# Batch 0 of a fused attention and feed-forward kernel: softmax with tokens on the partitions, sums of k and v two heads at a time, the first weights by columns

## The chip, the cores and the metric

The kernel runs on one core of one Trainium2 chip. The metric is the device time of one execution in microseconds, as the median of the runs shown. Engines are named as in the profile: PE (TensorE, matrix products), DVE (VectorE), ACT (ScalarE), POOL (GpSimd), SP (SyncE, which here only issues loads and stores).

## The reference

```
# q, k, v: 8 batches x 8 heads x 576 x 64; phi: 8 x 8 x 576 x 32; all float32
a = exp(phi - max(phi, axis=2));  a = a / (sum(a, axis=2) + 1e-9)     # softmax over the 576
k_m = einsum('bhsm,bhsd->bhmd', a, k);  v_m = einsum('bhsm,bhsd->bhmd', a, v)
s = (q @ k_m^T) / sqrt(64)                                            # 576 x 32 for each head
attn = exp(s - max(s, axis=-1));  attn = attn / (sum(attn) + 1e-9)    # softmax over 32 memory slots
x = (attn @ v_m), heads side by side                                  # 4608 x 512
h = x @ w_in                                                          # w_in 512 x 2048
out = max(0.01 * h, h) @ w_out                                        # w_out 2048 x 512
```

w_in and w_out arrive as 64-bit floats.

## The kernel before

**What is computed in which order.** For each batch the kernel sums k and v over the 576 positions with the weights exp(phi - max), which leaves 32 memory slots a head. It doesn't form attn @ v_m: v_m is multiplied into w_in first (the fold, `fold_products`), so that a token's 8 x 32 probabilities are multiplied by a folded matrix of 256 x 2048 straight away. The output is computed in units of tokens: `up_products` (L1248 early, L1378 later), the leaky relu, and `down` (L1335, later L1446) with w_out.

**Layout.** A batch has 8 heads in two groups `g` of four (`hh`). Positions lie on the partitions as 64 rows a group and nine columns `j` (KJ = 9, of which the first NJ = 6 are called early here). The array of PE is used in tiles: a product of 64 rows by 32 columns takes one of eight tiles, and products on different tiles run side by side. float32 products take two passes each.

**Order of the work.** All work is cut into named steps, and the strings OPENING and LATER list them. Every engine executes its share in that order. A step waits for what it reads and for the buffers that it writes. There are three kinds of PSUM buffers (`pa` three, `ph` two, `po` three banks). Loads go into eight slots of one arena in turn (`ld_slot`), or, for batch 0, into tiles that get their weights only later; eight semaphores are shared by the loads in turn.

**The steps of batch 0** (prefix `a0.`), with the lines of the profile before:

- `phi`, `k`, `v`, `q`: loads, from SP's queue, two of phi from ACT's. `T`: an exp of one column (L566), which brings ACT's table load with it. `z.n`: n idle products (L1538) into a fresh `po` tile; they compute nothing that is used.
- `A1` maximum of phi over positions (DVE L622), `A2` its transpose on PE (L663) and the maximum `mx` (L670), `A3` the identity scaled by mx, one half on DVE (L672), one on ACT (L673), `B0` PE spreads these over the partitions (L679), `B1` subtraction (DVE L688), `B2` exp (ACT L694), `B3` sums of the exponentials (DVE L710 to L719).
- `C10` sums of k (PE L738), `C11` sums of v (same line), `C2` and `C30` the divisor `r`, `C3k` and `C31` scaling to `x_k` (ACT L780) and `x_v` (ACT L810), `C4` a bound of x_v for later scalings.
- `D10`, `D3`: transposes of x_k (PE L833) and their copy to `kT` (ACT L868); `D11`, `D5`: the same for v (`vT`, L874). `R` and `Q`: transposes of q on PE (L933) and copies (DVE L942, ACT L944). `E10` to `E13`: scores (PE L979).
- `E2`: 32 x 32 transposes of the scores on DVE (L1030), so that the memory slots lie along the free axis; `S01` to `S08`: softmax over the slots, with a maximum (L1057), subtraction (L1060), exp (ACT L1065), sum (L1069 to L1071), product (L1074) and a second 32 x 32 transpose to `a` (L1082). `S1x` does the late positions.

`i0` to `i3` and `o0` to `o3` are quarters of w_in and w_out: `ld` loads a piece, `h` and `y` or `t` convert it (ACT L406 and L395, DVE L415, the put). `f0j.1` is the fold of quarter j (PE L1156), `f0j.2` its copy (ACT L1521), `u0.P0` the first product of tokens with folded weights. Batch 1 has its steps `a1.` spread among the units.

Of the kernel before, what the change touches and what calls it, by code (L numbers as in the profile page):

```python
# [31 lines left out]
EPS = 1e-09  # L32
# [7 lines left out]
a0.phi1 a0.phi2 z.2 z.2 z.2 z.2 z.2 a0.A12 a0.phi0 a0.phi3 a0.T a0.k3 a0.A10 a0.A11 z.2 z.2 a0.A13  # L40
a0.A2 a0.A3 z.2 a0.B0 a0.B11 z.2 z.2 a0.k2 a0.k0 a0.B10 z.2 a0.k1 z.2 a0.B21 a0.B20 a0.B12 a0.B30
a0.q3 a0.B31 a0.q1 a0.B22 a0.C100 a0.C101 a0.B32 a0.C102 a0.R3 a0.C2 a0.C30 a0.q2 a0.q0 a0.R1 a0.Q3
a0.C3k a0.R2 a0.Q2 i0.ld1 a0.Q1 a0.D10 a0.D3 a0.R0 a0.Q0 a0.E10 i0.y1 a0.E11 i0.h1 z.2 a0.E21 i0.ld0
z.2 z.2 i0.y0 a0.E20 z.2 z.2 a0.v0 z.2 a0.S01 a0.v1 z.2 a0.v2 z.2 a0.S02 a0.v3 i0.ld2 i0.h0 a0.C11
i0.t1 a0.S03 z.2 a0.q4 a0.q5 i0.t0 o0.ld1 o0.ld0 z.2 i1.ld0 a0.C31 i0.y2 a0.S04 a0.D11 a0.R5 i0.h2
a0.D5 a0.R4 a0.Q5 a0.S05 i1.ld1 i0.t2 a0.S06 a0.Q4 f00.1 a0.E12 f00.2 a0.E13 a0.C4 u0.P0 a0.E22 i0.b
u0.V0 u1.P0 a0.D2 o0.y0 u1.V0 u0.P1 u1.P1 o0.h0 a0.E23 o0.h1 i1.ld2 o0.ld2 a0.S11 i1.h0 o0.y1 o1.ld0
o1.ld1 u1.V1 a0.S12 a0.S13 i1.y0 u0.V1 o0.t0 a0.D4 i1.y2 i1.h1 i1.y1 o0.t1 o0.y2 o1.ld2 o0.h2 u0.O0
a0.S14 a0.S15 u1.O0 i1.h2 i1.t0 o2.ld0 a0.S16 o1.y0 o1.y1 o1.h0 i1.t1 i2.ld0 i1.t2 u0.O1 i2.ld1
f01.1 o0.t2 o1.h1 o1.t0 o1.y2 f01.2 u1.O1 i2.ld2 o1.h2 o1.t1 o2.y0 i2.h0 o1.t2 i2.h1 o2.ld1 u2.P0  # L50
u3.P1 a1.phi o2.ld2 a1.kv0 i2.y0 u2.V0 u2.P1 o2.h0 i2.y1 i2.y2 i2.h2 u2.V1 i2.t0 o2.y1 o2.t0 i2.t1
i2.t2 u2.O0 u3.V1 o2.h1 f02.1 a1.A1 f02.2 u3.P0 a1.kv1 o2.h2 a1.A2 u3.V0 a1.A3 o2.y2 a1.kv2 a1.kv3
u4.P1 o1.b o2.t1 a1.B0 a1.B10 a1.B20 u3.O0 a0.S17 u4.P0 i2.b o2.t2 a1.B3 i3.ld0 i3.h0 a1.C10 u4.V0
o0.b a1.C2 a1.C30 a1.q0 u2.O1 a1.C31 a1.q1 i3.ld1 a1.C3k i3.y0 i3.ld2 a1.D11 a1.D10 u4.V1 a1.D5
a0.S18 a1.C4 a1.D3 a1.D2 u5.P0 a1.Q0 a1.D4 u3.O1 i3.t0 o3.ld0 a1.Q1 i3.h1 a1.E1 a1.E20 i1.b u5.P1
u5.V0 o2.b o3.ld2 i3.y1 a1.E21 u4.O0 i3.y2 a1.S01 u5.O0 i3.h2 a1.S02 u5.V1 a1.E22 o3.y0 a1.S03 i3.t1
i3.t2 o3.h0 a1.S04 f03.1 o3.ld1 o3.y2 i3.b o3.h2 ci.1 a1.S11 u4.O1 a1.S05 o3.y1 a1.S06 o3.h1 o3.t0
a1.S12 o3.t2 f03.2 ci.2 o3.t1 a1.S13 o3.b a1.S07 u7.P0 ci.3 a1.S14 ci.4 u7.V0 w1.1 e. co.1 u6.P0
co.2 co.3 w0.2 a1.S08 u6.V0 u6.P1 co.4 e2. u7.P1 w1.2 a1.S15 a1.S16 u6.V1 o0.k2 u6.O0 u7.V1 u7.O0
o0.k0 o0.l0 u5.O1 o0.k1 o0.l1 u6.O1 a1.S17 a1.S18  # L60
# [10 lines left out]
o0.l2 u7.O1 W01.h1 a2.phi a2.kv2 a2.kv1 o0.s0 W01.h0 a2.A1 Z0.0 o0.s1 a2.kv0 a2.A2 W01.l0 o0.m0  # L71
W01.l1 o0.m1 o0.n0 o0.n1 Z0.1 o0.s2 i0.k1 W11.p Z0.2 P8.0 P8.1 V8.0 a2.kv3 W11.h1 P9.0 o0.s3 V8.1
# [114 lines left out]
def kernel(  # L187
# [96 lines left out]
    for g in range(2):  # L284
        nc.gpsimd.memset(sides[g * 64:(g + 1) * 64, g:g + 1], 1.0)
    junk = wi[0].bitcast(BF16)[:, 0:WC]
# [77 lines left out]
    w_out_v = w_out.rearrange("(j p f) e -> j p (f e)", p=P, j=NQ)  # L364
    PIECES = [(c0, min(PC, WC - c0)) for c0 in range(0, WC, PC)]

    def weights(kind, j, steps, act):
# [4 lines left out]
        src, dst, split, col = src[j], dst[j + 1], split[j], slice(col, col + 1)  # L372
# [3 lines left out]
        def load(i):  # L376
# [3 lines left out]
            if kind == "o":  # L380
                nc.sync.dma_start(st[:, 0:n], src[:, c0:c0 + n])
                x = c0 + n
# [27 lines left out]
        def put(i):  # L410


            hi, lo, _ = words.pop(i)
            c0, n = PIECES[i]
            nc.vector.scalar_tensor_tensor(  # L415
                dst.bitcast(U32)[:, c0:c0 + n], hi, 3, lo, ALU.logical_shift_left, ALU.bitwise_or
            )
# [100 lines left out]
    def attention(b, steps, chunks, f32_chunks=0):  # L518
# [29 lines left out]

        def load_kv(hh, kinds):
            if ("ld", hh) not in ld:  # L550
                n = 4 * 2 * KJ * D
                t = ld["ld", hh] = (
                    (wo[2], wo[3], wo[4], wi[4])[hh] if b == 0
                    else ld_slot() if b == 1 else at(n * hh, n)
                )
                ld["kv", hh] = t[:, 0:2 * KJ * D].rearrange("p (i j d) -> p i j d", i=2, j=KJ)
# [32 lines left out]
        def load_pairs(x):  # L589
            hs, js = (slice(x, x + 1), slice(0, NJ)) if x < HP else (  # L590
                slice(2 * x - 2 * HP, 2 * x - 2 * HP + 2), slice(NJ, KJ)
            )
            s = hs.start // 2
            if ("q", s) not in ld:
                ld["q", s] = ld_slot()[:, 0:2 * KJ * D].rearrange(
                    "p (hh j d) -> p hh j d", hh=2, j=KJ
                )
# [103 lines left out]
        def sum_phi(x):  # L701
# [6 lines left out]
            t = wi[3][:, n:n + HP * 2 * M].rearrange("p (hh j m) -> p hh j m", hh=HP, j=2)  # L708
            if x == 0:
                nc.vector.tensor_tensor(t[:, :, 0], ph[:, :, 0], ph[:, :, 1], ALU.add)  # L710
                return
            if x == 1:
                nc.vector.tensor_tensor(t[:, :, 1], ph[:, :, 2], ph[:, :, 3], ALU.add)
                nc.vector.tensor_tensor(t[:, :, 0], t[:, :, 0], ph[:, :, 4], ALU.add)
                return
            s0 = var["s0"] = att.tile([P, HP, M], F32, name="r1k", bufs=2)
            for j in (5, 7):
                nc.vector.tensor_tensor(t, t, ph[:, :, j:j + 2], ALU.add)
            nc.vector.tensor_tensor(s0, t[:, :, 0], t[:, :, 1], ALU.add)  # L719
# [7 lines left out]
        def slots_of(kinds, js=range(KJ)):  # L727
# [5 lines left out]
            cs = slice(kinds[0] * D, (kinds[-1] + 1) * D)  # L733
            for j in js:
# [18 lines left out]
        def _():  # L753
            s0 = var["s0"].rearrange("p hh m -> p (hh m)")
            if b == 0:
                nc.tensor.matmul(var["pk"][0][:, P:P + NG], s0, sides, start=True, stop=True)
# [5 lines left out]
        def _():  # L762
            var["r2"] = r = sm.tile([P, NG], F32, name="r2")
            sums_ = var["pk"][0][:, P:P + NG]
# [9 lines left out]
        def _():  # L774
            x_k = att.tile([P, NG, ND, NB, 32], F32, name="x_k")
            if b == 0:
                flat = x_k.rearrange("p g db tb x -> p (g db tb x)")
                var["x_k"] = flat[:, 0:NG * P].rearrange("p (g i d) -> p g i d", g=NG, i=2)
                for g in range(NG):
                    nc.scalar.activation(  # L780
                        var["x_k"][:, g],
                        var["pk"][g][:, 0:D].unsqueeze(1).broadcast_to([P, 2, D]),
                        AF.Copy, scale=var["r2"][:, g:g + 1],
# [41 lines left out]
        def _():  # L825
# [4 lines left out]
            if b == 0:  # L830
                var["pkT"] = pkT = ps_a.tile([P, NG, P], F32, name="pa")
                for g in range(NG):
                    nc.tensor.transpose(  # L833
# [804 lines left out]
```

## Time and profile before

| | us |
|---|---|
| median of 3 runs | 653.81 |
| lowest and highest | 653.44, 656.79 |
| the profiled execution, time | 656.04 |
| the profiled execution, span | 654.2 |
| PE busy in it | 637.7 |
| DVE busy | 513.3 |
| ACT busy | 393.8 |
| first product of tokens (u0.P0) | 28.49 |

The span is the profiled part of one execution, from its first to its last instruction. Busy is time in which an engine had an instruction in work; idle products count as busy, and a view by stretches and the chain of waits show where PE works for nothing. The clock granted to PE was full throughout.

### The profile page before, as it was taken

The page shows a single profiled execution, that of the slowest core. Times are in us where ns is not written, and L with a number is a line of the kernel's source. Part 1 is how long each engine was busy: PE and PEld are TensorE (multiplying, and loading weights), DVE is VectorE, ACT ScalarE, POOL GpSimd, SP SyncE. Part 2 cuts the span into 40 slices and gives each one's busy share as a digit, 9 for nine tenths or more (in the row PEclk, how much of TensorE's full clock was granted, in tenths as well). Part 3 has the DMA queues.
Part 4 walks back from the last instruction along what each step waited for, and adds up shares of the span by engine and source line. Part 5 has one row for each costly group of instructions (what it writes and reads, how often), then busy time and mean ns, then how long its engine had stood idle before and what let it go on. Part 6 is the DMA issues. An engine that isn't in the chain of part 4 may idle for free.

```text
span 654.2 us, 17243 instructions
## 1 busy us (share of the span) xinstructions
PE 637.7 (97%) x7317; PEld 482.8 (74%) x7317; DVE 513.3 (78%) x856; ACT 393.8 (60%) x682; POOL 30.1 (5%) x41
## 2 busy tenths in 40 slices
PE   8999999999999999999999999999998999999997
PEld 4545445665546778888888888887877888889896
DVE  4677898998987898899869975789886897575641
ACT  4599977764554555467546665655574466564543
POOL 0000130000010001002000010000010001000000
PEclk9999999999999999999999999999999999999999
DMA  9899814014602644421253011164114010010102
GB/s 319 320 367 317 289 36 122 10 22 89 193 10 36 136 142 82 120 88 41 35 130 127 3 32 42 26 120 146 33 27 79 12 33 18 17 28 7 33 1 50
DMA packets 85885, 61.17 MB, mean 93 GB/s; under 512 B 62128, under 2 KB 69040, under 8 KB 85808
## 3 DMA queue, kind: packets, MB, share of 16 engines
q1 hardware_dynamic: 85328, 59.64, 32.4%
q8 instruction: 57, 0.93, 0.6%
q10 hardware_dynamic: 480, 0.43, 0.2%
q14 instruction: 20, 0.16, 0.1%
HBM read 50.59 MB, written 9.45 MB: 92 GB/s over the span
## 4 chain that ended last, share of the span: by engine, by line
PE 92%; DVE 2%; ACT 2%; issue 1%; DMA 1%; SPq 1%; POOL 0%; ACTq 0%; DVEq 0%; POOLq 0%
PE po L1446 30%; PE ph L1378 21%; PE po L1335 15%; PE ph L1248 8%; PE ph L1446 5%; PE pa L1156 4%; PE pa L738 3%; PE po L1538 2%; PE po L1481 1%; PE pa L963 1%; SPq L587 1%; DMA arena<-in_moe_w_out_dram 1%; ACT wi L1394 1%; PE po L738 1%; DMA arena<-in_q_dram 0%
## 5 line engine op out<-in xcount | busy, mean ns | idle before, releaser
L1446 PEld LDWEIGHTS <-arena 128*128 128x128 f16 x2184 | 209.8, 98 | 35.0 <-issue 11.9
L1394 ACT ACTIVATE wi<-ph,g_sc 128x256 f32<-128x256 f32 (+1 forms) x224 | 99.0, 464 | 167.5 <-PE ph L1378 160.5
L1378 PE MATMUL ph<-a,w_mem 128*128 128x256 f16 (+3 forms) x1440 | 145.3, 246 | 3.6 <-ACT wi L1394 3.6
L1378 PEld LDWEIGHTS <-w_mem 128*128 128x128 f16 x1440 | 114.6, 98 | 17.9 <-issue 7.2
L1446 PE MATMUL po<-wo,arena 128*128 128x256 f16 x936 | 122.2, 273 | 0.9 <-issue 0.9
L1446 PE MATMUL po<-arena 128*128 128x256 f16 x936 | 122.2, 273 | 0.0
L1335 PE MATMUL po<-wo,arena 128*128 128x512 f16 (+1 forms) x384 | 109.5, 433 | 0.0
L1423 DVE TENSOR_TENSOR arena<-arena 128x1024 f16<-128x1024 f32 x52 | 63.5, 1221 | 23.0 <-ACT arena L1419 23.0
L1423 DVE TENSOR_TENSOR arena<-wi,arena 128x768 f16<-128x768 f32 (+1 forms) x60 | 54.6, 910 | 10.1 <-ACT arena L1419 10.1
L1415 DVE TENSOR_TENSOR arena<-wi 128x256 f32<-128x256 f32 x104 | 40.4, 428 | 26.3 <-ACT wi L1394 25.7
L1419 ACT CAST arena<-arena 128x1024 f16<-128x1024 f32 x52 | 54.4, 1046 | 9.6 <-DVE arena L1415 9.4
L1248 PE MATMUL ph<-a,w_mem 128*128 128x192 f16 (+2 forms) x304 | 52.0, 317 | 0.0
L1335 PEld LDWEIGHTS <-arena 128*128 128x128 f16 x288 | 27.8, 98 | 29.8 <-issue 0.6
L1419 ACT CAST arena<-wi 128x768 f16<-128x768 f32 (+1 forms) x60 | 46.6, 776 | 1.6
L1415 DVE TENSOR_TENSOR arena<-wi,arena 128x256 f32<-128x256 f32 x104 | 45.6, 438 | 1.8
L1446 PE MATMUL ph<-wo,arena 128*128 128x256 f16 x312 | 42.6, 273 | 1.8 <-issue 1.8
L1121 POOL TENSOR_TENSOR a<-t,a 128x128 f16<-128x128 f32 (+3 forms) x17 | 21.9, 1305 | 464.1 <-ACT a L1116 458.3
L1335 PEld LDWEIGHTS po<-wo,arena 128*128 128x128 f32 x96 | 17.9, 190 | 21.0 <-issue 19.4
L1156 PE MATMUL pa<-wi,vT 64*32 64x512 f16 (+1 forms) x704 | 29.4, 420 | 0.0
L1255 ACT ACTIVATE arena<-ph,g_sc 128x384 f32<-128x384 f32 x32 | 18.5, 581 | 15.7 <-PE ph L1248 15.4
L1248 PEld LDWEIGHTS <-w_mem 128*128 128x128 f16 x240 | 20.7, 98 | 9.7 <-issue 3.6
L1189 ACT ACTIVATE w_mem<-pa 128x512 f16<-128x512 f32 x40 | 22.7, 595 | 8.5 <-PE pa L1156 7.4
(226 smaller groups left out, 761.7 us busy)
## 6 DMA issues: line engine op xcount, KB each, us to landing
out_dram<-obs SPq DMA_DIRECT2D x140, 64.0 KB, 1.7
arena<-in_k_dram SPq DMA_DIRECT2D x28, 288.0 KB, 4.4
arena<-in_v_dram SPq DMA_DIRECT2D x28, 288.0 KB, 5.1
arena<-in_q_dram SPq DMA_DIRECT2D x96, 72.0 KB, 2.9
arena<-in_moe_w_in_dram SPq DMA_DIRECT2D x12, 512.0 KB, 6.9
arena<-in_moe_w_out_dram SPq DMA_DIRECT2D x8, 768.0 KB, 8.4
arena<-in_phi_dram SPq DMA_DIRECT2D x7, 576.0 KB, 4.7
arena<-in_moe_w_in_dram SPq DMA_DIRECT2D x8, 256.0 KB, 6.3
```

What stands on the lines that cost most here:

```text
L738: nc.tensor.matmul(var["pk"][g][hh * M:(hh + 1) * M, cs], ld["phi"][rows, hh, j, :], ld["kv", hh][rows, kinds[0]:kinds[-1] + 1, j, :], sta ...
L1121: nc.gpsimd.tensor_tensor(piece(lo, tb), piece(t2, tb), piece(hi, tb), ALU.subtract)
L1156: nc.tensor.matmul(pf[g][cols, :], lhs, rhs, start=(n == 0), stop=(n == len(passes) - 1), tile_position=(g * D, hh * M),)
L1189: nc.scalar.activation(tiles(halves(w16(b, j), g)[:, 0]), w(g), AF.Copy, scale=ws)
L1248: nc.tensor.matmul(ph[:, t0:t0 + n * SB], lhs, rhs, start=(m == 0), stop=(m == len(seq) - 1))
L1335: nc.tensor.matmul(po, lhs, rhs, start=(f == 0 and m == 0), stop=(f == NQ * NF - 1 and m == len(seq) - 1),)
L1378: nc.tensor.matmul(ph[:, t0:t0 + n], lhs, rhs, start=(m == 0), stop=(m == len(seq) - 1))
L1394: nc.scalar.activation(dst, ph, AF.Prelu, scale=g_sc2[:, j:j + 1], alpha=SLOPE)
L1415: nc.vector.tensor_tensor(gt[:, x], y, z, op)
L1419: nc.scalar.copy(dst[:, 0], src)
L1423: nc.vector.tensor_tensor(dst[:, 1], src, dst[:, 0], ALU.subtract)
L1446: nc.tensor.matmul(acc, g[:, x, s, u], rhs, start=(h == 0 and j == 0 and u == 0 and m == 0), stop=(j == NQ - 1 and u == 1 and m == 2), ski ...
```

## The change

The kernel's first 30 us are rewritten for batch 0, and the two lists of steps with them. In detail:

- **Loads.** The order is phi, q1, k, q0, a first part of v, q3, q2, the rest of v, then the first piece of w_in, the late q in one load, the other two pieces of w_in, and w_out's first quarter by rows. k and v are loaded as pairs of heads. The late q takes two of the arena's slots, one for its transposes.
- **Warm-up.** `a0.T` stands behind `a0.A3`. 13 idle products stand at the start; all idle products write one tile (`idle_sums`). There are 9 ahead of the sums of k and none ahead of the sums of v.
- **Sums.** `C10` and `C11` are 36 products each, of two heads' weights (64 columns) with two heads' values (128 columns), of which the diagonal blocks are used. The exponentials are written to a tile of their own with the heads innermost.
- **Scaling of x_v** is shared: ACT takes one half, DVE the other.
- **Scores.** q is the stationary side and kT the moving one, so that the tokens come out on the partitions and the memory slots along the free axis. kT is cleared by POOL at the start (`K`) and written by eight small copies (`D3`). `score_rows` and `late_scores` take the place of `scores_of`; the steps `E2` fall away for batch 0.
- **Softmax** (`by_rows`) in three parts: two early columns (`T0`), four early columns (`S0`), three late ones (`S1`). The maximum and the subtraction read PSUM directly. PE transposes the probabilities, and one copy each on ACT and DVE brings them to `a`.
- **First quarter of w_in** in pieces of 128, 192 and 192 of its 512 columns, each converted, folded (`fold_part`) and copied on its own, the copy half on ACT and half on DVE. w_out's first quarter uses another assignment of rows to the partitions, so that the first fold's columns are contiguous.
- **Later steps** of the opening and the start of LATER are in another order. Among them: the products of u6 and u7 stand elsewhere around `co.1` to `co.4` (where PE waits for DVE at L498), and four late steps of batch 1 move behind the opening.

The core of the diff (the lists of steps are cut to the first lines):

```diff
 OPENING = """
-a0.phi1 a0.phi2 z.2 z.2 z.2 z.2 z.2 a0.A12 a0.phi0 a0.phi3 a0.T a0.k3 a0.A10 a0.A11 z.2 z.2 a0.A13
-a0.A2 a0.A3 z.2 a0.B0 a0.B11 z.2 z.2 a0.k2 a0.k0 a0.B10 z.2 a0.k1 z.2 a0.B21 a0.B20 a0.B12 a0.B30
...
+z.1 a0.K z.2 a0.phi1 z.1 z.2 z.1 z.1 z.1 z.1 z.1 z.2 a0.phi2 a0.phi0 a0.q1 a0.A12 a0.R1 a0.phi3
+a0.A11 a0.k1 a0.k2 a0.k0 z.2 a0.k3 a0.A10 a0.A13 a0.A2 z.2 a0.A3 a0.T z.2 a0.B0 a0.Q1 z.1 z.2 z.2
+a0.B10 a0.B20 a0.B11 a0.B12 a0.B21 a0.q0 z.2 a0.B30 a0.v3 a0.q3 a0.B31 a0.q2 a0.v1 a0.B22 z.2 a0.v0
...
+    COLUMNS = [(0, P), (P, 320), (320, FQ)]
...
+            if by_columns:
+                x0, x1 = COLUMNS[i]
+                n = NC * (x1 - x0)
+                x = c0 + n
+                nc.sync.dma_start(
+                    st[:, 0:n].rearrange("p (c f) -> p c f", c=NC), src[:, :, x0:x1]
+                )
...
+            if x == HP:
+                n = HP * (KJ - NJ) * D
+                ld["q_late"] = ld_slot()[:, 0:n].rearrange("p (hh j d) -> p hh j d", hh=HP, d=D)
+                ld["qT_late"] = ld_slot()[:, 0:2 * HP * P].rearrange("p (k x) -> p k x", k=2)
+                nc.sync.dma_start(ld["q_late"], src[:, :, NJ:KJ])
+                return
...
+            if b == 0:
+                i = kinds[0]
+                for j in js:
+                    for hp in range(HP // 2):
+                        for g in range(NG):
+                            rows = slice(g * D, (g + 1) * D)
+                            nc.tensor.matmul(
+                                var["pk"][g][hp * D:(hp + 1) * D, i * P:(i + 1) * P],
+                                phi_of(slice(0, KJ))[rows, j, 2 * hp:2 * hp + 2, :].rearrange(
+                                    "p hh m -> p (hh m)"
+                                ),
+                                ld["pair", i, hp][rows, :, j, :],
+                                start=(j == 0), stop=(j == KJ - 1), tile_position=(g * D, hp * D),
+                            )
+                return
...
+            for to, q_of, rows, n in pairs:
+                for hh in range(HP):
+                    for g in range(NG):
+                        half = slice(g * D, (g + 1) * D)
+                        nc.tensor.matmul(
+                            to[half, :, hh], q_of[rows, hh, g], var["kT"][rows, g, hh, 0:n],
+                            start=True, stop=True, tile_position=(0, g * D),
+                        )
...
+            def s1():
+                t1()
+                nc.vector.tensor_reduce(one("tm"), scores_(), AX.X, ALU.max)
+
+            def s2():
+                nc.vector.tensor_tensor(t1(), scores_(), all_of("tm"), ALU.subtract)
+
+            def s3():
+                nc.scalar.activation(t1(), t1(), AF.Exp)
+
+            def s4():
+                nc.vector.tensor_reduce(one("ts"), t1(), AX.X, ALU.add)
+                nc.vector.tensor_scalar(one("ts"), one("ts"), EPS, 1.0 / A_SCALE, ALU.add, ALU.mult)
+                nc.vector.reciprocal(one("ts"), one("ts"))
+
+            def s5():
+                eng = nc.vector if x < 2 else nc.gpsimd
+                eng.tensor_tensor(t1(), t1(), all_of("ts"), ALU.mult)
...
+                    nc.tensor.transpose(
+                        to[j], t1()[:, j * HP:(j + 1) * HP].rearrange("p hh m -> p (hh m)"), ident
+                    )
...
+            def s7():
+                if x < 2:
+                    nc.scalar.copy(*early(0))
+                    return
...
+            def s8():
+                if x < 2:
+                    nc.vector.tensor_copy(*early(1))
+                    return
...
+    def fold_part(x0, x1):
+        pf = first["f", x0] = [ps_o.tile([P, x1 - x0], F32, name="po") for g in range(NG)]
+        for hh in range(HP):
+            for g in range(NG):
+                rows, cols = slice(g * D, (g + 1) * D), slice(hh * M, (hh + 1) * M)
+                nc.tensor.matmul(
+                    pf[g][cols, :], states[0]["vT"][rows, cols],
+                    wi[1][rows, hh * FQ + x0:hh * FQ + x1], start=True, stop=True,
+                    tile_position=(g * D, hh * M),
+                )
+
+    def keep_part(x0, x1):
+        nc.scalar.copy(w32[0][0][:, x0:x1], first["f", x0][0])
+        nc.vector.tensor_copy(w32[0][1][:, x0:x1], first["f", x0][1])
...
-    def idle_products(n):
-        pi = ps_o.tile([P, NF, P], F32, name="po")
+    idle_sums = []
+
+    def idle_products(n, f32):
+        if not idle_sums:
+            idle_sums.append(ps_o.tile([P, NF, P], F32, name="po"))
...
         for _ in range(n):
+            nc.tensor.matmul(idle_sums[0], by, of, start=True, stop=True)
```

Three places as the engines get them. What stands in brackets is what an instruction waits for. First ACT's start, before:

```order
L547 DMA wi_88<-in_phi_dram 128x288 x2
L566 ACT_TABLE_LOAD
L566 ACTIVATE sq<-ones 128x1 [waits Pool_49]
L673 ACTIVATE r1k<-ident,mx_148 128x128 [waits DVE_49,Pool_49]
L694 ACTIVATE wi_88<-wi_88 128x4x96 [waits DMAHW2_49,DMAHW1_49,DMAHW3_49,DMAHW0_49,DVE_49]
```

The same in the new program, where L703 is the scaled identity of A3, L596 the warm-up exp and L726 the exp of phi:

```order
L567 DMA wi_88<-in_phi_dram 128x288 x2
L703 ACT_TABLE_LOAD [waits DVE_49]
L703 ACTIVATE r1k<-ident,mx_159 128x128 [waits Pool_49]
L596 ACTIVATE sq<-ones 128x1
L726 ACTIVATE wo_90<-wo_90 128x256 [waits DVE_49]
```

The table load stood free at the start; now it stands behind A3's wait for DVE's mx. Second PE, between the scores of batch 0 and the sums of v, before (the last two of 16 idle products, and the first sums; wo_92 holds v):

```order
L1538 LDWEIGHTS ones
L1538 MATMUL po<-ones 128x512 [waits PE_49]
L1538 LDWEIGHTS ones
L1538 MATMUL po<-ones 128x512
L738 MATMUL po<-wo_92,wi_88 32x64 [waits DMAHW0_49]
L738 MATMUL po<-wo_92,wi_88 32x64
```

And in the new program (L1073 are the scores by rows, L777 the sums, wo_94 and wi_89 hold v):

```order
L1073 MATMUL pa<-kT,wi_87 64x2x32 [waits PE_49]
L1073 MATMUL pa<-kT,wi_87 64x2x32 x15
L777 MATMUL po<-wo_94,wo_90 64x128 [waits DMAHW6_49,DMAHW5_49]
L777 MATMUL po<-wo_94,wo_90 64x128
L777 MATMUL po<-wi_89,wo_90 64x128 [waits DMAHW7_49,DMAHW2_49]
```

The idle products between scores and sums of v are gone, and a product is 64 x 128 for 32 x 64. Third DVE, from the scaling of x_v to `a`, before:

```order
L1074 TENSOR_TENSOR t_322<-t_322,ts__449 128x768 [waits DVE_49]
L415 SCALAR_TENSOR_TENSOR wi_86<-arena 128x512 [waits DMAHW4_49,Activation_49]
L1082 STREAM_TRANSPOSE a<-t_322 128x768 [waits DVE_49]
L818 TENSOR_REDUCE l_506<-x_v 128x2
L346 TENSOR_REDUCE m_509<-l_506 128x1 [waits DVE_49]
```

And in the new program (L873 is DVE's half of x_v, L1253 to L1259 the softmax, L435 the puts of w_in, L883 to L353 the bound of x_v, L1290 the copy of the transposed probabilities to `a`):

```order
L873 SCALAR_TENSOR_TENSOR x_v<-po,wo_90,x_v 128x64 [waits Activation_49] x2
L1253 TENSOR_REDUCE ts__305<-t_303 128x16
L1254 TENSOR_SCALAR ts__305<-ts__305 128x16 [waits DVE_49]
L1255 RECIPROCAL ts__305<-ts__305 128x16 [waits DVE_49]
L435 SCALAR_TENSOR_TENSOR wi_86<-arena 128x4x128 [waits DMAHW0_49]
L1259 TENSOR_TENSOR t_303<-t_303,ts__305 128x512 [waits DVE_49]
L883 TENSOR_REDUCE l_422<-x_v 128x2
L351 TENSOR_REDUCE m_425<-l_422 128x1 [waits DVE_49]
L353 TENSOR_SCALAR mdiag<-ident,m_425 128x128 [waits DVE_49]
L435 SCALAR_TENSOR_TENSOR wi_86<-arena 128x4x192 [waits DMAHW2_49,Activation_49]
L1290 COPY a<-ph 128x384 [waits PE_49]
```

The sum and the normalization of the softmax, which stood ahead of anything from v, now stand behind x_v, with two puts among them.

More of the change, by code (lines that the diff above doesn't have):

```diff
@@ L50 @@
[L50 to L55, printed above, removed]
@@ L285 @@
         nc.gpsimd.memset(sides[g * 64:(g + 1) * 64, g:g + 1], 1.0)
+    parity = wo[0][:, 2:4]
+    nc.gpsimd.memset(parity, 0.0)
+    for x in range(4):
+        nc.gpsimd.memset(parity[x * 32:(x + 1) * 32, x % 2:x % 2 + 1], 1.0)
     junk = wi[0].bitcast(BF16)[:, 0:WC]
@@ L830, in _ @@
             if b == 0:
-                var["pkT"] = pkT = ps_a.tile([P, NG, P], F32, name="pa")
+                var["pkT"] = [ps_a.tile([P, P], F32, name="pa") for g in range(NG)]
                 for g in range(NG):
-                    nc.tensor.transpose(
-                        pkT[:, g, :], var["x_k"][:, g].rearrange("p i d -> p (i d)"), ident
-                    )
+                    nc.tensor.transpose(var["pkT"][g], var["x_k"][:, g], ident)
                 return
@@ L917, in flip_q @@
             )
-        for g in range(HP + 2 if b == 0 else NG):
+        for g in range(HP + 1 if b == 0 else NG):
             steps[f"{name}q{g}"] = lambda g=g: load_q(g)
@@ L1011, in attention @@
         if b == 0:
-            for g in range(NG):
-                steps[f"{name}E1{g}"] = lambda g=g: scores_of(0, g, (0, 1))
-            for i in range(2):
-                steps[f"{name}E1{2 + i}"] = lambda i=i: [scores_of(1, g, (i,)) for g in range(NG)]
+            for x in range(2):
+                steps[f"{name}E1{x}"] = lambda x=x: score_rows(x)
+                steps[f"{name}E1{2 + x}"] = lambda x=x: late_scores(x)
         else:
@@ L1039, in flip @@
             )
-        for tb in range(NB + 1 if far or b == 0 else NB):
+        for tb in range(0 if b == 0 else NB + 1 if far else NB):
             steps[f"{name}E2{tb}"] = lambda tb=tb: flip(tb)
@@ L1132, in a_f32 @@
+        if b == 0:
+            for key, x, j0, j1 in (("S0", 0, 0, NF), ("T0", 1, NF, NJ), ("S1", 2, NJ, KJ)):
+                by_rows(key, x, j0, j1)
+        else:
+            for c, (b0, b1) in enumerate(chunks):
+                chunk(c, b0, b1, c < f32_chunks)
     def a_f32(b):
@@ L1515 @@
         opening(u)
-    for j in range(NQ):
+    for j in range(1, NQ):
         def products(j=j):
@@ L1520 @@
         steps[f"f0{j}.2"] = lambda j=j: [
-            nc.scalar.copy(tiles(w32[j][g]), by_tile(first["f", j][g])) for g in range(NG)
+            nc.scalar.copy(tiles(w32[j][g]), by_tile(first["f", j][g], j)) for g in range(NG)
         ]
+    def fold_part(x0, x1):
+        pf = first["f", x0] = [ps_o.tile([P, x1 - x0], F32, name="po") for g in range(NG)]
+        for hh in range(HP):
+            for g in range(NG):
+                rows, cols = slice(g * D, (g + 1) * D), slice(hh * M, (hh + 1) * M)
+                nc.tensor.matmul(
+                    pf[g][cols, :], states[0]["vT"][rows, cols],
+                    wi[1][rows, hh * FQ + x0:hh * FQ + x1], start=True, stop=True,
+                    tile_position=(g * D, hh * M),
+                )
+    def keep_part(x0, x1):
+        nc.scalar.copy(w32[0][0][:, x0:x1], first["f", x0][0])
+        nc.vector.tensor_copy(w32[0][1][:, x0:x1], first["f", x0][1])
+    for x, (x0, x1) in enumerate(COLUMNS):
+        steps[f"f00.{2 * x + 1}"] = lambda x0=x0, x1=x1: fold_part(x0, x1)
+        steps[f"f00.{2 * x + 2}"] = lambda x0=x0, x1=x1: keep_part(x0, x1)
     for kind in "io":
```

281 lines of the change are left out of this document (184 added, 97 removed).

## The prediction

> **What bounds the kernel now.** I read the page's totals first, then a table of the opening by stretches (length, busy time and count of each engine, the clock granted to PE, DMA share, GB/s), then the chain of waits there.
>
> ```profile
> PE 637.7 (97%) x7317; PEld 482.8 (74%) x7317; DVE 513.3 (78%) x856; ACT 393.8 (60%) x682; POOL 30.1 (5%) x41
> ```
>
> ```profile
> 10.00:16.80 6.80, 4.89 (x171) 3.47 (x160) 2.58 (x8) 5.01 (x10) 0.00 (x0) 1.00 1.02 366
> 16.80:22.00 5.20, 4.80 (x37) 1.58 (x43) 5.06 (x7) 1.03 (x2) 0.00 (x0) 1.00 1.05 398
> 22.00:28.40 6.40, 5.98 (x205) 4.00 (x193) 4.58 (x10) 3.70 (x10) 0.00 (x0) 1.00 0.70 239
> 28.40:60.00 31.60, 31.60 (x123) 14.90 (x115) 22.00 (x32) 30.41 (x49) 2.99 (x4) 1.00 1.01 369
> ```
>
> PE is busy 97% of the span. From 28.40 on it has no gap for 30 us, so what other engines can set is mainly the stretch ahead of the first product of tokens with folded weights (L1248). PE is shown busy there too, but much of that is idle products (L1538), which compute nothing. What the change can win or lose is therefore read from this chain; its columns are start, duration and work:
>
> ```profile
> 6.95 0.30 DVE r1k L672
> ...
> 7.82 1.83 PE po L1538 x8
> 9.65 1.59 PE po L738 x100
> 11.25 0.49 PE ph L933 x3
> ...
> 13.65 0.57 DVE wi L942
> ...
> 14.35 0.87 PE pa L979 x29
> 15.22 1.10 issue
> 16.32 0.51 PE pa L979 x3
> 16.84 0.55 PE po L1538 x2
> ...
> 21.91 1.25 PE po L738 x81
> 23.16 0.18 issue
> 23.88 1.00 PE po L1538 x4
> ...
> 25.87 1.10 PE pa L1156 x14
> ...
> 28.49 1.81 PE ph L1248 x5
> ```
>
> The sums of k end at 11.24 and the scores at 16.84. Then 16 idle products take 5.07 us (16.84 to 21.91), the sums of v end at 23.88, and the fold leads to 28.49. The 5.07 us are the prize. They bridge the time until v is there, which is issued behind w_in:
>
> ```profile
> 10.89 0.59 SPq L558 DMA_DIRECT2D wi<-in_v_dram  x1
> wi<-in_v_dram SPq DMA_DIRECT2D x1, 288.0 KB, 7.4
> ```
>
> The second row's last number is from issue to landing, so the last of v is there at 18.3 (10.89 + 7.4).
>
> **The terms, in order of time**, each a change in when a thing ends.
>
> 1. Ahead of the first reduction (A2) stand 13 idle products, three transposes of q and two idle products, where 14 idle ones stood. Idle products are 0.23 apart when warm (1.83 / 8), and three transposes take 0.49 less some 0.1 of overlap: -0.2 + 0.4 + 0.4 = +0.6.
>
> 2. The warm-up exp moves behind step A3, and ScalarE's table load goes with it. Before, it ran while phi was still coming:
>
> ```profile
> 1.67 1.28 ACT L566 ACT_TABLE_LOAD   x1 [1.67 <-PEq L1622]
> 2.96 0.20 ACT L566 ACTIVATE sq<-ones 128x1 f32<-128x1 f32 x1
> 6.94 0.40 ACT L673 ACTIVATE r1k<-ident,mx 128x128 f32<-128x128 f32 x1 [3.77 <-DVE mx L670]
> 13.32 0.38 ACT L868 ACTIVATE kT<-pa 128x256 f32<-128x256 f32 x1
> ```
>
> In the new program the load is ScalarE's first instruction behind its two phi DMAs, and it carries the wait for DVE's mx. Its 1.28 us then lie wholly between mx and the 0.40 of the scaled identity, for which PE's second broadcast product waits, behind that DVE's subtraction, the exp and the sums of k: +1.3, so +1.9 so far. The copy of q on DVE (0.57) that now stands before the subtraction lies under the load, and would cost its 0.57 if the load were free. The Trainium skill, in "ScalarE: Activation LUTs", section "What ACT_TABLE_LOAD costs", gives 1283 ns for the load and a drain of about 1380 ns behind it. The trace agrees with the first and shows no second, as the next instruction starts when the load ends (1.67 + 1.28, 2.96). By the page the total would be 1.4 us more, an estimate.
>
> 3. Nine idle products follow where eight did. They all write one tile now, so that none waits for a buffer, which saves about what the ninth costs: 0. The sums of k start at 11.5.
>
> 4. These become 36 products of 128 columns in four tiles of the array, for 72 of 64 columns in eight; a tile has 18 passes in both. The nearest rows are later batches' sums, which have 128 columns already:
>
> ```profile
> 60.37 2.18 PE pa L738 x144
> 202.92 2.68 PE pa L738 x142
> ```
>
> Against 1.59 that is +0.6 at most, and with half the instructions 0 at least; +0.4 taken, nearer to the wide row. The sums end at 13.5.
>
> 5. From there to the scores it was 3.1 us (11.25 to 14.35), and the last wait was for a copy of q (13.65, 0.57). Now kT is written by four small copies on ScalarE and four on DVE at the same time. At 0.25 each, between the 0.20 and the 0.38 of the rows under 2, they take 1.0 for 0.38. That is +0.6 on a branch that was 0.5 early (13.32 + 0.38, against 14.22): 3.1 again, scores from 16.6.
>
> 6. The scores by rows are 24 products of 64 columns for 16 of 192. The old ones took 0.87 + 0.51 = 1.38 besides their wait. Bounds 1.3, and 2.6, where two tiles at a time instead of eight halve the rate; 2.0 taken, in the middle. They end at 18.6 (16.84 before, with the wait of 1.10).
>
> 7. No idle product stands behind them, and v's loads stand ahead of w_in's, about five loads of 288 KB earlier at 366 to 398 GB/s, so that v is there. The sums of v start at 18.6 instead of 21.91: -3.3.
>
> 8. They take 1.9 like those of k, if nothing stops them. But PE waited twice in the chain for "issue", nothing that the profile shows: 1.10 and 0.18. Both waits end 2.4 to 2.5 us after a packet of the instruction queue, which two stretches of the DMA view show (13.8 to 14.2 and 20.8 to 21.2; the columns are packets, MB, share):
>
> ```profile
> q8 instruction: 1, 0.02, 15.5%
> q8 instruction: 1, 0.02, 17.3%
> ```
>
> I read them as blocks of instructions that come late because loads are queued ahead of them; this is an inference. Counted along PE's program, the two places are 256 instructions apart, and by the same count the new order meets the next one two thirds through the sums of v, 19.9, with the block asked for at 13.5. Bounds: 0; and 1.7, if the packet stands behind the 2 MB that SP may then have queued (5.6 us at 366 GB/s) and takes 2.5 more, 21.6. I take 1.1, the row that is nearest in place. The sums end at 21.6 (23.88 before).
>
> 9. From there to the first product of tokens it was 4.61. The new path runs on DVE, priced by
>
> ```profile
> 19.82 1.82 DVE L415 SCALAR_TENSOR_TENSOR wi<-arena 128x768 uint32<-128x768 uint32 x2
> 21.56 0.94 DVE L1069 TENSOR_REDUCE ts__449<-t 128x24 f32<-128x768 f32 x1
> 22.53 0.18 DVE L1070 TENSOR_SCALAR ts__449<-ts__449 128x24 f32<-128x24 f32 x1
> ```
>
> x_v behind ScalarE's half of it, 0.7; the sum over slots 0.63 (0.94 x 512/768); a put of w_in 0.6 and one of 0.9 (by size from 1.82 / 2); the normalization, of as many elements, 0.64; five small ones between 0.18 and 0.30, 1.2; the copy of the transposed probabilities 0.57: 5.2. The first product is at 26.8, 1.7 earlier. The softmax is queued behind x_v on DVE, so whatever delays the sums of v delays it in full.
>
> 10. Work that stood ahead of that product and now stands behind: the last piece of the fold (192 columns of 512 of its 16 products, 1.10 x 16/14 x 192/512 = 0.5) and three transposes of the late probabilities (0.5, as three of q took at 11.25). +1.0: net -0.7.
>
> 11. By the count of 8, two blocks begin within batch 1's sums, one soon after the other. The rows under 4 show such a burst without and with a delay, 0.5 apart. Bounds 0 and 1.5; +0.8 taken.
>
> 12. Later the trace has one wait for DVE that stands among moved steps:
>
> ```profile
> 71.08 4.29 DMA arena<-in_moe_w_out_dram
> PE pa L498 <- DVE diag L492: 0.9, 1, 0.9
> ```
>
> The chain goes from the last load of w_out through ScalarE and DVE to PE at 87.31. The new order puts more products ahead of that, but the loads are reordered too. Bounds -0.9 and +0.9, 0 taken.
>
> POOL's added memset runs at the start, under the phi loads; two more load slots held by the late q are in 12. PE's remaining work is the same. Sum: -0.7 + 0.8 = +0.1. The profiled execution took 656.04, the median of the runs is 653.81: 656.1 and 653.9.
>
> **The rivals.**
>
> Faster: blocks of instructions come in time. Then -1.1 and -0.8 fall away, with scores at 1.3 another -0.7, and with the wait of 12 gone -0.9: -3.4 in all, 650.4. "Runtime: NRT & Kernel Launch" of the Trainium skill, section "Instruction fetch mechanics", calls the crossing of a block mostly hidden; 2.18 at 60.37 agrees, 1.10 at 15.22 doesn't. Against this rival speaks that loads run at 366 GB/s or more just when the block is asked for.
>
> Slower: the last load of w_out lands later. PE at 87.31 waits for its chain already, so each us of delay is one at the end. The place is the queue's pause for free slots: 0.70 in 22.00:28.40 leaves 1.9 us without loads. The late q now takes one slot for itself and one for its transposes, and the second comes free only behind the late scores, which stand behind the sums of v. Loads issued by then (some 2 MB from 13.5 on, and the first two pieces of w_out) are through by 20 to 23; if the next is issued at 25 to 28, the pause is 5.2 us, 3.3 more than now: 657.2. It decides from a pause 1 us longer. Against it: the 0.9 of 12 may come with cover, as more products stand ahead of it, and what lands late in one place was early in another, w_in's first quarter.
>
> No effect: the opening ends earlier or later by 2 us, but ScalarE, 30.41 of 31.60 busy from 28.40 on, sets when the later steps are ready, and the difference comes back as waits of PE: 653.8. Against it: PE has no gap there now.
>
> **Chances.** About 0.5% (3.3 us) is what a measurement of this kernel can tell from no change. The sum with middle values, 651 to 656.5, has 0.41, no effect 0.15; the faster rival, at or near its end, 0.24; the slower one 0.20. Sum and no effect both count as no change. The range takes in the ends of the rivals.
>
> **What would show it.** The table load near 7.5; sums of k from about 11.5; scores near 16.6; the sums of v right behind, with a wait for "issue" inside; the first product of tokens between 26 and 28; a burst of 2.7 us or more near 60. I am wrong if the table load is off the chain, if the sums of v run through, if PE waits for ScalarE between 30 and 60, or if the wait at 87 grows.

## The result and the profile after

The changed kernel takes 657.85 us (median of 9 runs, 656.38 to 662.41), the kernel before 655.16 in the same comparison (9 runs, 653.44 to 658.12). The ratio, taken over all nine of each, is 1.0055, 95% interval 1.0034 to 1.0076: slower by 0.55% (0.41% by the medians), where 653.9 was forecast. Four executions of the experiments below took 738 us or more, far above all others, and are left out of the ranges and ratios.

The two profiled executions don't show this difference as a whole: 656.38 with a span of 654.1 after (the lowest of its nine), 656.04 with 654.2 before (above its median). They do show where each gains and loses, and the comparisons of total time below are made by timed runs.

The opening, from the chain of waits of the changed kernel (start, duration, work; L693 is the transpose ahead of the maximum mx, L1737 are idle products, L777 the sums, L1073 the scores, L1422 the products of tokens, L1703 the fold's pieces):

```profile
6.56 0.12 PE pa L693
...
7.09 1.28 ACT L703
8.38 0.41 ACT r1k L703
...
9.27 2.05 PE po L1737 x9
11.32 2.13 PE po L777 x72
...
16.01 1.98 PE pa L1073 x48
17.99 2.13 PE po L777 x72
...
25.12 0.61 PE po L1703 x16
25.74 1.49 PE ph L1422 x4
```

The table load lies on the chain as forecast. The sums of v follow the scores at once and run through. The first product of tokens starts at 25.74, 2.75 us earlier than 28.49. That is the largest value of this gain: in the profiles of five runs below with the same opening it starts at 25.87 to 26.57, as the transpose L693 starts anywhere between 6.56 and 7.40. All of the gain and more is lost 31 us later, in batch 1's sums of k and v (L790):

```profile
57.07 2.27 PE pa L790 x135
59.34 2.56 issue
61.90 0.65 PE pa L790 x7
62.54 0.41 PE pa L812
62.95 2.52 PE ph L1422 x4
...
68.82 1.29 PE ph L1422 x4
```

PE waits 2.56 us with 7 passes of the burst left. What follows it is slow too: four passes of L1422 take 2.52 at 62.95 and 1.29 at 68.82. The view by stretches shows why; the last three columns are the granted clock, the DMA share and GB/s:

```profile
56.00:59.30 3.30, 3.30 (x140) 2.26 (x138) 3.12 (x3) 3.30 (x5) 0.00 (x0) 1.00 1.07 302
59.30:61.90 2.60, 0.04 (x4) 0.00 (x1) 0.00 (x0) 2.17 (x3) 0.00 (x0) 1.00 0.12 29
61.90:65.30 3.40, 3.40 (x12) 1.82 (x13) 2.03 (x9) 1.20 (x3) 0.00 (x0) 0.50 0.41 104
65.30:70.00 4.70, 4.70 (x18) 2.44 (x16) 3.00 (x4) 2.56 (x5) 0.00 (x0) 1.00 0.99 362
```

After the wait PE had half its clock for 3.4 us. That costs 1.2 in L1422 (2.52 less 1.29), 0.5 in the last passes of L790 (0.65 for some 0.1) and 0.15 in L812 (0.41 for the 0.26 of a run without the wait): about 1.9 us on top of the 2.56. By the first of the later products of tokens the changed kernel is 1.92 us behind; the rows of before and after:

```profile
104.36 4.07 PE ph L1248 x48
```

```profile
106.28 3.96 PE ph L1422 x48
```

The waits of PE for "issue" in the whole program (total, times, longest), before and after:

```profile
PE ph L1446 <- issue: 1.8, 1, 1.8
PE pa L979 <- issue: 1.1, 1, 1.1
PE po L1446 <- issue: 0.9, 1, 0.9
PE pa L738 <- issue: 0.3, 1, 0.3
PE po L738 <- issue: 0.2, 1, 0.2
```

```profile
PE pa L790 <- issue: 5.1, 3, 2.6
```

Both kernels have such waits in or behind bursts of sums of later batches, but in different places: 2.56, 1.39 and 1.19 after (59, 206, 423 us), 0.3, 0.9 and 1.8 before (141, 249, 495). A burst is the row of some 290 short instructions of PE that makes a batch's sums of k and v; an extra or idle product is one that computes nothing that is used. The wait of 0.9 for DVE at L498 is gone.

### The profile page after: what moved, and what is told of

Same layout as the page of the kernel before. It is cut to its first block, busy times and chain, and to the rows that moved or that the text cites. A ratio compares the mean times of both kernels' runs of the same rounds, so it can differ in the third digit from the quotient of the medians.

```text
span 654.1 us, 17083 instructions
## 1 busy us (share of the span) xinstructions
PE 639.5 (98%) x7222; PEld 486.4 (74%) x7222; DVE 514.9 (79%) x869; ACT 394.8 (60%) x687; POOL 30.3 (5%) x44
## 4 chain that ended last, share of the span: by engine, by line
PE 95%; DVE 1%; issue 1%; ACT 1%; DMA 1%; SPq 0%; ACTq 0%; DVEq 0%
PE po L1620 31%; PE ph L1552 22%; PE po L1509 16%; PE ph L1422 8%; PE ph L1620 5%; PE pa L1329 4%; PE pa L790 3%; PE po L1655 1%; PE pa L1047 1%; PE po L1737 1%; ACT wi L1568 1%; PE po L777 1%; DMA arena<-in_q_dram 1%; PE pa L1073 0%; DVE r1k L741 0%
## 5 line engine op out<-in xcount | busy, mean ns | idle before, releaser
L1597 DVE TENSOR_TENSOR arena<-wi,arena 128x768 f16<-128x768 f32 (+1 forms) x60 | 54.6, 911 | 10.1 <-ACT arena L1593 10.1
L1422 PE MATMUL ph<-a,w_mem 128*128 128x192 f16 (+2 forms) x304 | 53.4, 322 | 0.0
L1212 POOL TENSOR_TENSOR a<-t,a 128x1024 f16<-128x1024 f32 (+2 forms) x15 | 21.3, 1435 | 433.2 <-ACT a L1207 433.2
L1329 PE MATMUL pa<-wi,vT 64*32 64x512 f16 (+1 forms) x688 | 27.8, 416 | 0.0
L1422 PEld LDWEIGHTS <-w_mem 128*128 128x128 f16 x240 | 20.7, 98 | 9.4 <-issue 3.3
```

Of the source, the lines that this page charges most:

```text
L1212: nc.gpsimd.tensor_tensor(piece(lo, tb), piece(t2, tb), piece(hi, tb), ALU.subtract)
L1329: nc.tensor.matmul(pf[g][cols, :], lhs, rhs, start=(n == 0), stop=(n == len(passes) - 1), tile_position=(g * D, hh * M),)
L1422: nc.tensor.matmul(ph[:, t0:t0 + n * SB], lhs, rhs, start=(m == 0), stop=(m == len(seq) - 1))
L1597: nc.vector.tensor_tensor(dst[:, 1], src, dst[:, 0], ALU.subtract)
```

## The experiments

Theory A was that the lost time is instruction supply: PE's program comes in blocks of 256 instructions, and two boundaries of blocks lie inside batch 1's burst. Its rival B put the time elsewhere, above all into the table load. All ratios are to the kernel before on the same chip, with 95% intervals.

**16 extra products ahead of the burst (64 PE instructions).** In `fold_products`, for quarter 1, each real product is preceded by two of 8 columns in its own tile, which the real one overwrites:

```diff
+                    for _ in range(2 if b == 0 and j in (1,) and hh * NG + g < 16 else 0):
+                        nc.tensor.matmul(
+                            pf[g][cols, 0:8], lhs, rhs[:, 0:8], start=True, stop=True,
+                            tile_position=(g * D, hh * M),
+                        )
```

> The changed kernel with 16 extra products of 8 columns in the fold of quarter 1 (64 PE instructions, about 0.3 us of work), all ahead of batch 1's sums of k and v. Theory A (two block boundaries of PE's program lie inside that burst of sums, so the second block comes late): the first boundary now lies some 3 us ahead of the burst, the 2.56 us wait for 'issue' at 59 us and the halved clock behind it (62 to 65) are gone, 3.5 to 4.5 us are won: 653.5 to 654.5, ratio to the kernel before 0.997 to 1.000. Theory B (the time went elsewhere: the table load on the chain, more work after the opening, the loads): no gain, 657.9 to 658.5, ratio 1.005.

Measured: 1.0007 (0.998 to 1.0034), with single runs between 652.25 and 658.68 us. Three of these, with a mean granted clock of 0.999 or 1.000, took 652.25 to 653.96; the other seven, with 0.995 to 0.997, took 656.74 to 658.68. The extra products cost 1.3 us and not 0.3, probably because they kept the real ones from running side by side. The profiled execution is one of the seven (658.37), and in it the wait didn't go:

```profile
58.59 1.82 PE pa L790 x102
60.41 3.63 issue
64.04 1.50 PE pa L790 x39
```

So A as put doesn't explain this execution: one boundary was now some 40 instructions ahead of the burst, and the wait grew. By count PE passed that boundary at 52.6. Yet the next packet of the instruction queue is seen only between 61 and 62:

```profile
q8 instruction: 1, 0.02, 7.4%
```

**The same products behind the burst** (`j in (3,)`).

> Control: the changed kernel with the same 16 extra products, but in the fold of quarter 3, behind batch 1's sums. Theory A: the burst is where it was, the wait of about 2.5 us and the halved clock stay, +0.3 us of work: ratio to the kernel before 1.005 to 1.007. Theory B: the same as the other placement, ratio 1.005.

Measured: 1.0032 (1.0017 to 1.0046), with a wait of 3.35 us at 59.46. The wait stays, as A said; the placement ahead gave 0.25% less, and the two intervals overlap.

**The same products in the kernel before.**

> The kernel before with the same 16 extra products in the fold of quarter 1. They move batch 1's sums to where two block boundaries lie inside them, at 9% and 96%, as in the changed kernel. Theory A: a wait of 1 to 2.6 us for 'issue' appears at the end of that burst near 63 us, with a halved clock behind it if it is over 2 us: 2 to 4 us slower, ratio 1.003 to 1.006. Theory B: only the 0.3 us of added work, ratio 1.000 to 1.001.

Measured: 1.0052 (1.0032 to 1.0072), as A's number said, but only in part for its reason. The wait in batch 1's burst is 0.6 us, and the clock stayed full there. Two later bursts wait too, so that the waits now stand in the same three bursts as in the changed kernel:

```profile
66.94 0.60 issue
...
209.53 1.11 issue
...
425.45 1.75 issue
```

They sum to 3.5 us, for 3.1 in other bursts of the kernel before. The extra products cost 1.3 us here too. This profiled execution also lost 3.1 us in the opening, whose program is unchanged (first product of tokens at 31.63 for 28.49):

```profile
15.88 1.26 issue
17.14 0.85 PE pa L979 x3
17.99 0.98 PE po L1543 x2
```

```profile
15.00:20.00 5.00, 3.67 (x36) 1.22 (x37) 1.94 (x3) 2.54 (x4) 0.00 (x0) 0.71 1.05 393
20.00:25.00 5.00, 4.66 (x12) 1.30 (x11) 4.86 (x8) 0.84 (x1) 0.00 (x0) 0.61 0.98 390
```

After 1.26 us (1.10 in the first profile) the clock was halved for 6.8 us (0.29 and 0.39 of 5 us each are missing from the clock, over 0.5), and pairs of idle products took 0.98 instead of 0.55. That isn't what makes the 0.5%: seven of the ten executions had a mean granted clock of 0.999 or 1.000, and their median is 657.37 us. The products and the waits account for 1.7 us; the rest stays open.

**The warm-up exp at the front.**

```diff
-a0.A11 a0.k1 a0.k2 a0.k0 z.2 a0.k3 a0.A10 a0.A13 a0.A2 z.2 a0.A3 a0.T z.2 a0.B0 a0.Q1 z.1 z.2 z.2
+a0.A11 a0.k1 a0.k2 a0.k0 z.2 a0.k3 a0.A10 a0.A13 a0.A2 z.2 a0.A3 z.2 a0.B0 a0.Q1 z.1 z.2 z.2
```

(and `a0.T` behind `a0.phi3` one line above)

> The changed kernel with the warm-up exp, and with it ScalarE's table load, at the front again. The sums of k start 1.2 to 1.4 us earlier (9.9 to 10.1 instead of 11.3). Theory A: that gain shows in the first product of tokens (24.4 instead of 25.7) and, as the late block at 59 stays, ratio to the kernel before 1.003 to 1.004. Theory B: if the table load is what made the kernel slower, ratio 1.000 to 1.002; if the chain is bound elsewhere (by v's scaling or w_in's first piece) the first product of tokens stays at 25.7 and the ratio at 1.005.

Measured: 1.0023 (1.0007 to 1.0038), against 1.0055 (1.0034 to 1.0076) with the load on the chain. The load ran at 1.67 again:

```profile
1.67 1.28 ACT L596 ACT_TABLE_LOAD   x1 [1.67 <-PEq L1819]
2.97 0.20 ACT L596 ACTIVATE sq<-ones 128x1 f32<-128x1 f32 x1
```

From the transpose to the sums of k it is now 3.47 us and not 4.76 (6.56 to 11.32), the 1.3 us that were expected:

```profile
7.38 0.11 PE pa L693
...
10.85 2.13 PE po L777 x72
```

The times themselves missed the expectation, 10.85 for 9.9 to 10.1 and a first product of tokens at 25.26 for 24.4, as the transpose came 0.82 us later in this execution. The ratio is as A said. The gain makes up less than the loss, and the wait of the burst stayed (2.81 us at 58.85): B's main suspect is a real cost, but not the one that turned the result.

Theory C came from the first of these runs: the next block is asked for only when PE has read some way, perhaps 60 instructions, into the current one, and PE can't read on past what waits at the start of the burst. Theory D: the block waits until batch 1's loads of q have drained.

**32 extra products (128 instructions)**, in one row ahead of quarter 1's fold, so that they run side by side:

```diff
+        for x in range(32 if (b, j) == (0, 1) else 0):
+            hh, g = x // NG % HP, x % NG
+            rows, cols = slice(g * D, (g + 1) * D), slice(hh * M, (hh + 1) * M)
+            nc.tensor.matmul(
+                pf[g][cols, 0:8], vT[rows, cols], wi[2][rows, hh * FQ:hh * FQ + 8],
+                start=True, stop=True, tile_position=(g * D, hh * M),
+            )
```

> The changed kernel with 32 extra products of 8 columns (128 PE instructions, about 1.4 us) ahead of the fold of quarter 1. The earlier shift by 64 left the wait (3.63 us), so theory A in its first form is wrong. Theory C: the next block of PE's program is fetched only once PE has read some 60 instructions into the current one, and it then needs 2.5 us and its turn behind loads; with the shift by 64 that point (963 + 60) was still inside the burst, 21 instructions after its start, with 128 it is 43 instructions ahead of it, some 3 us or more. So no wait in the burst or one under 1 us, no halved clock at 60 to 70: -4.4 + 1.4 = 3 us faster than the changed kernel, ratio to the kernel before 0.999 to 1.002. Theory D (the block waits until the loads of batch 1's q have drained, wherever it is asked for): the wait of 2 to 4 us stays, ratio 1.005 to 1.008.

Measured: 0.9945 (0.9925 to 0.9965), 651.89 us: 6 us less than the changed kernel (by the medians of two comparisons), with products added that compute nothing. The extra products took 0.61 us, the burst runs through, and one wait for "issue" is left in the program:

```profile
37.76 0.61 PE pa L1323 x46
...
58.48 2.46 PE pa L790 x142
```

```profile
PE ph L1429 <- issue: 0.5, 1, 0.5
```

The wait in the burst is gone, as C said and D didn't, with the loads of q the same. The ratio is below C's range: C had counted 3 us for batch 1 alone, and the later waits (1.39 and 1.19) are gone too.

**Float32 idle products.** `z.f`, a float32 idle product, in place of four short ones, and four left out behind the sums of v, which moves everything 33 instructions the other way:

```diff
-z.1 a0.K z.2 a0.phi1 z.1 z.2 z.1 z.1 z.1 z.1 z.1 z.2 a0.phi2 a0.phi0 a0.q1 a0.A12 a0.R1 a0.phi3
+z.1 a0.K z.f a0.phi1 z.f z.f a0.phi2 a0.phi0 a0.q1 a0.A12 a0.R1 a0.phi3
...
```

> The changed kernel with most idle products as float32 products (twice the time for the same number of instructions, so that they take as long), and without the four idle products behind the sums of v: batch 1's sums stand 33 instructions earlier in PE's program, and the second boundary falls 20 instructions behind them, some 4 us after the first block's 60th instruction. Theory C: no wait in or behind the burst, clock full: 4 to 4.5 us less than the changed kernel, ratio 0.997 to 0.9995. Theory D: the wait stays, perhaps behind the burst (2 us or more between 60 and 65): ratio 1.003 to 1.006.

> The same with the warm-up exp at the front, so that the table load is off the chain. With the 0.3% that the exp alone gave: theory C 0.994 to 0.997, 651 to 653 us, faster than both kernels; theory D 1.000 to 1.003.

Measured: 1.0032 (1.0014 to 1.0051) and, with the exp at the front, 0.9991 (0.9971 to 1.001). Both missed C's numbers, and the first lies in D's range, though not for D's reason: the wait in batch 1's burst did go, but others came; of the first of the two:

```profile
PE pa L790 <- issue: 2.7, 2, 1.6
PE pa L1329 <- DVE wi L435: 1.5, 1, 1.5
PE po L1620 <- issue: 1.1, 1, 1.1
```

The waits for "issue" are in later batches (249, 423 and 497 us, and one of 0.6 at 206), and PE waits for w_in's conversion at 73. C had been applied to one burst only. The second had 1.6 us in batch 0's sums of v, the wait that the prediction had feared there.

**Loads of batch 1's q behind a piece of w_in.**

```diff
-u5.P0 u2.O1 i3.ld2 a1.C3k
+u5.P0 u2.O1 i3.ld2 a1.q0 a1.q1 a1.C3k
```

> The changed kernel with the loads of batch 1's q issued behind one of w_in's last pieces, which waits for a slot until about 62 us; PE's program is the same. Theory D: without those loads in the queues at 57 to 59 the block arrives 1 to 1.5 us sooner, the wait in the burst is 1.0 to 1.5 us instead of 2.56 and the clock stays full or is halved for less long; q is late, so PE waits for its transposes at about 70 us for 0 to 4 us. Theory C without a part for the loads: the wait stays at 2.0 to 2.6 us. The total isn't told apart by this, the wait at 59 us is: ratio between 1.002 and 1.010.

Measured: 1.0043 (1.0028 to 1.0058), and the wait at its place:

```profile
59.84 3.04 issue
```

The piece of w_in found a free slot at 54.69, so that loads were in the queues as before. So this doesn't tell what part the loads have in the 2.5 to 3.6 us.

**The same place in the blocks for both kernels.** The change takes 181 instructions out of PE's program. With 180 extra ones (45 products in the loop above) the changed kernel's later bursts stand in their blocks as the kernel before has them. With 204 (51 products) the kernel before has them as the changed kernel with 128.

> The changed kernel with 45 extra products (180 PE instructions, 0.9 us): everything behind it then stands in the 256-instruction blocks of PE's program where it stands in the kernel before. Theory C, for the whole program: the wait at 59 stays away, but the kernel before's late ones come instead (0.3 near 141, 0.9 near 249, 1.8 near 495): 2.5 to 3.5 us more than with 128, ratio to the kernel before 0.998 to 1.001. Theory E (only batch 1's burst matters, because loads run beside it): like the shift by 128, 0.994 to 0.996.

> The kernel before with 51 extra products (204 PE instructions, 1 us) ahead of its fold of quarter 1: everything behind stands in the blocks where the changed kernel with 128 more has it. Theory C: no wait for 'issue' of 0.4 us or more behind 28 us, 3.1 us of waits less and 1.0 us of work more: ratio 0.996 to 0.998. What then is left between this and the changed kernel with 128 is the change's own part: 1 to 1.5 us. Theory E: +1 us of work and no gain, ratio 1.001 to 1.002.

Measured: 0.9984 (0.9967 to 1.0001) for the changed kernel with 180, and 0.9974 (0.9955 to 0.9994) for the kernel before with 204. The waits for "issue" of the first are those of the kernel before, near 248 and 494:

```profile
PE ph L1627 <- issue: 1.6, 1, 1.6
PE po L1627 <- issue: 0.6, 1, 0.6
```

Those of the second are the opening's and one of 0.5:

```profile
PE pa L979 <- issue: 1.1, 1, 1.1
PE ph L1255 <- issue: 0.5, 1, 0.5
```

So the waits go with the place in the blocks, through the whole program, and E falls. Products that compute nothing made the kernel before 0.26% faster.

All profiles together show the same. Counted in PE's records (weight loads, products, semaphore instructions), all waits for "issue" of 0.2 us and more stand at places that are whole multiples of 256 instructions apart, give or take one. The thirteen profiles have 91 bursts of sums in batches 1 to 7. In 28 of them a boundary lies 4 to 50 instructions behind the burst's start, and each of the 28 waits at the next boundary, inside or just behind the burst, for 0.4 to 3.4 us. Of the other 63 only three wait: 0.3 and 1.6 us with a boundary 4 instructions ahead of the start, and the 3.63 us in batch 1 with one some 40 ahead. The halved clock goes with the waits: in all 24 executions of the changed kernel with 128 or 180 more instructions the mean granted clock was 0.999 or 1.000, in eight of nine of the changed kernel 0.995 to 0.997.

Whether the change is a gain by itself, at equal places, isn't shown. The ratios point that way, 0.9945 against 0.9974 (0.3%, 1.9 us) and 0.9984 against 1 (0.16%, 1 us), but the first two intervals overlap and the third takes in 1. In the second comparison, too, 12 of the kernel before's 23 executions had a mean clock of 0.997 or less; the other 11 have a median of 654.26 us, against 654.45 for the changed kernel with 180.

**128 extra instructions and the exp at the front.**

> The changed kernel with 128 more instructions and the warm-up exp at the front: the waits stay away and the table load's 1.3 us go too, unless the sums of v wait for their second block because they come earlier (1.6 us in one run with the exp at the front): ratio 0.992 to 0.995, the fastest so far if below 0.9945.

Measured: 0.9927 (0.9904 to 0.9951), 650.52 us, the fastest of all and faster than both kernels. Its chain has the sums of k at 10.44 and no wait in any sums:

```profile
10.44 2.13 PE po L777 x72
...
17.11 2.12 PE po L777 x72
...
24.85 1.49 PE ph L1429 x4
```

## Why the prediction was wrong

The forecast of the opening held within about 1 us, and the sum failed at its term 11: the wait for a block in batch 1's sums, taken at 0.8 us, cost about 4.5 with the halved clock behind it.

- Terms 1 to 3 (sums of k at 11.5): 11.32. From the transpose on they took 1.51 us more than before (4.76 for 3.25), where 1.3 was put: 1.28 for the load, and 0.22 for the ninth idle product (2.05 for 1.83), which term 3 put at 0; term 1's +0.6 was +0.16 in this profile (6.56 for 6.40), and another profile of the same opening has 1.0. The table load measured 1.28 on the chain, and the instruction behind it started 0.01 us after its end (7.09 + 1.28, 8.38), so the drain of 1380 ns that the Trainium skill adds ("ScalarE: Activation LUTs", section "What ACT_TABLE_LOAD costs") isn't seen here either.
- Terms 4 to 7: the sums of k took 2.13 (1.99 assumed), the scores started at 16.01 (16.6) and took 1.98 (2.0), the sums of v started at 17.99 (18.6).
- Term 8, 1.1 us for a late block in the sums of v: 0 here. The block came in time, though one variant had 1.6.
- Term 9, the first product of tokens at 26.8: 25.74. Without the 1.1 of term 8 and with the 0.6 of earlier sums the forecast would have been 25.1, so the path behind the sums of v took 5.6 us and not 5.2. It isn't the path of the term either: in the chain of this profile it is PE's throughout (20.12 to 25.74), with four idle products among its work, and not DVE's. In the run with float32 idle products and the exp at the front, which leaves these four out, the chain does go over DVE, and takes 5.24 us (20.98 to 26.22).
- Term 10 (+1.0) wasn't measured alone. What is left of the 1.92 us at 106 after -2.75, +2.56, +1.9 and -0.9 is 1.1.
- Term 11, +0.8 for two boundaries in batch 1's sums: the right place and cause, mis-sized. It was 2.56 of wait and 1.9 of halved clock. The two rows used for it, 2.18 and 2.68, aren't a burst without and with a delay: both bursts have one boundary and no wait, and in the profiles the bursts of batches 3 to 5 that don't wait take some 2.6 to 2.7, and those of batches 1, 2, 6 and 7 some 2.2 to 2.5. The upper bound of 1.5 for the wait was also too low, and the clock wasn't in the sum at all.
- Term 12: the wait is gone, -0.9, the lower of the bounds given.
- Behind 87 us the sum has nothing ("PE's remaining work is the same"), which was the other fault. The change moves every later instruction within its block, so that all later bursts count: by the profiles 2.6 us of waits after (1.39 and 1.19) against 3.1 before (0.3, 0.9, 1.8). Here the two nearly balance, which is luck.

Of the rivals none came true as told. The slower one named w_out's last load; there was no such wait. The table load was taken into the sum at full price but not drawn as a fault to be undone; the three pairs of runs with and without it on the chain differ by 0.2 to 0.4%. The sentence of "Runtime: NRT & Kernel Launch" of the Trainium skill (section "Instruction fetch mechanics") that a crossing is mostly hidden fits the products of tokens, where no wait stands at the boundaries away from the bursts, and not the bursts of sums, where waits of up to 3.6 us were measured.

Open: how far into a block PE must be before the next is asked for, and how much of the wait the loads make. The 60 instructions are read from when packets come, not measured by themselves, and they don't fit everywhere: in the kernel before a packet comes at 138.77, ahead of a burst that starts at 139.06, though the boundary lies only 4 instructions ahead of that burst. Open too is the sum of the whole: in the two profiled executions the changed kernel is 1.92 us behind at 106 and 0.1 ahead at the end, of which the later waits for "issue" explain 0.5, while the medians of the timed executions are 2.7 us apart. What shows that instruction supply turned the sign is the runs with 128 and 180 extra instructions, not this sum.

## What to carry to other kernels

Where an engine issues bursts of hundreds of short instructions, count where the burst stands in the 256-instruction blocks of its program: a change that adds or removes instructions anywhere ahead moves every later burst, and a few useless ones in the right place can be worth more than the change. Here a burst of some 290 instructions that begins 4 to 50 instructions ahead of a boundary always cost a wait, and any other hardly ever (3 of 63). Judge a change at equal places, or try it with some small shifts, before calling it slower. And put the first activation, which brings the table load, where nothing waits for it.

## What the runs showed of the hardware

A wait of PE can cost more than its length. After 2.56 us without products the granted clock was 0.50 for 3.4 us; after 3.63 us it was still 0.50 between 68 and 70. In the run with float32 idle products and the exp at the front, a wait of 2.07 us for w_in's conversion (73.4 to 75.5) was enough (the last three columns are clock, DMA share and GB/s):

```profile
76.30:79.80 3.50, 2.94 (x12) 1.17 (x5) 3.40 (x8) 3.43 (x7) 2.47 (x2) 0.51 0.21 74
```

After 0.74 and 1.26 us with 0.87 of work between them the clock was halved for 6.8 us in one execution, while 0.74 and 1.10 in another left it full, and so did 1.39 and 1.82 alone. The Trainium skill ("TensorE: Matmul & The Clock Gate", section "Part 1: The HAM clock gate (the "warmup" mystery)") puts the drop at an idle window of about 3.4 us; here waits of 2.07 and 2.56 us were enough.
